# First pair fetched uncast, q pooled one pair ahead, filler matmuls and a ring of six in a fused attention and gated-unit kernel

## The chip, the cores and the metric

One core of one Trainium2 chip runs the whole program. The metric is the device time of one execution in microseconds (us), the median of several runs.

In the text PE is TensorE, DVE is VectorE, ACT is ScalarE, POOL is GpSimd and SP is SyncE.

## The reference, cut to what matters

```python
# q, k, v: (8 batches, 8 heads, 1152, 64) float32, values about 0.1
q_pool = q.reshape(B, H, S // 2, 2, D).mean(axis=3)            # (8, 8, 576, 64)
attn   = softmax(q_pool @ k.T / sqrt(D))
x      = (attn @ v) laid out as (8, 576, 512)
gate   = sigmoid(causal 5-tap convolution of x along the sequence, per channel)
out    = (gate * (x @ w_val)) @ w_out                           # (8, 576, 512) float32
```

Scores are small, so the kernel expands the softmax to first order: per head it needs a 64x64 product of k and v (a Gram matrix) and column sums, not the scores. A flag computed at the end sends the program to an exact version if the inputs are too large. That never happens here.

## The kernel before

Heads are handled in 32 pairs, four pairs to a batch. I call the work for one pair a **slot**, numbered 0 to 31. Slot n computes the Gram matrix of pair n, x of pair n-1, and a quarter of the gated unit ("MoE" in the names) of the batch before. So slots 0 to 3 have no MoE work, and slot 4 is the first full one. "First slot of a batch" below means slots 4, 8, 12 and so on, "second slot" 5, 9, 13 and so on.

```python
def load_pair(n):                 # ring of NKV = 7; GpSimd's DMA casts float32 to bf16
    t = kvs[n % NKV]
    nc.gpsimd.dma_start(out=qn, in_=q[...])
    nc.gpsimd.dma_start(out=t[:, W:2 * W]..., in_=k[...])
    nc.gpsimd.dma_start(out=t[:, 0:W]..., in_=v[...])
# ... (cut)
def pool_q(n):                    # DVE: sum of neighbouring rows of q
    nc.vector.tensor_tensor(out=qp, in0=qv[..., 0, :], in1=qv[..., 1, :], op=ALU.add)
def transposes(n):                # PE: 6 transposes of qp into qt_ps; ACT: copy to mq
    ...
    nc.scalar.copy(out=mq[:, 2 * D:]..., in_=qt_ps...)
# ... (cut)
pool_q(0); transposes(0); setup_conv(); pool_q(1)
for n in range(NPAIR):
    # loads up to pair n + 6; w_val and w_out behind pair 3
    grams(n)                      # PE: sm (18 matmuls), then g (18 matmuls)
    rows(n)                       # DVE
    if late is not None:
        gval(*late)               # DVE: gate times value, left over from slot n-1
    if after:
        xhat(n - 1); xevac(n - 1) # PE; ACT
    rank1(n)                      # PE, needs rows(n)
    if after: norms(n - 1, g)     # PE
    if n >= 2: tap(n - 2, 2)      # DVE: third tap of the convolution
    stat(n, g)                    # DVE
    # ACT: scaled copy of g to mq
    if n >= 2: gate(n - 2)        # ACT: sigmoid
    if moe: mA = val(...) if slot < 2 else outs(...)      # PE
    if n + 2 < NPAIR:
        pool_q(n + 2)             # DVE: two pairs ahead
    if moe: gval(...) if slot < 2 else oevac(...)         # DVE; ACT
    if n + 1 < NPAIR: transposes(n + 1)                   # PE, ACT
    if after: conv(n - 1); tap(n - 1, 0); tap(n - 1, 1)   # PE; DVE
    squares(n)                    # ACT
    if moe: mB = val(...) or outs(...)   # PE; in slot < 2 its gval becomes "late"
```

Each engine executes its instructions in this order.

## Time and profile before

The median is 185.86 us (185.73 to 186.06, 3 runs). The profiled execution took 185.47 us, a little less than these; its span, from the first to the last instruction, is 183.6 us.

| stage of the kernel before | from, to (us) | what sets its pace |
|---|---|---|
| slots 0 to 3 | 9.83 to 33.66 | arrival of the pairs, and the wait for q |
| slot 4, at half clock | 33.66 to 39.43 | PE |
| slots 5 to 31, 18.4 us per batch | 39.43 to 164 | PE |
| tail: last batch of MoE, stores, flag | 164 to 183.6 | PE, then the last stores |

A line of a timeline has the start, the duration, engine, source line, operation and tiles; the bracket is the idle time of that engine just before, and what ended it.

### The profile page before, as it was taken

The page shows a single profiled execution, that of the slowest core. Times are in us where ns is not written, and L with a number is a line of the kernel's source. Part 1 is how long each engine was busy: PE and PEld are TensorE (multiplying, and loading weights), DVE is VectorE, ACT ScalarE, POOL GpSimd, SP SyncE. Part 2 cuts the span into 40 slices and gives each one's busy share as a digit, 9 for nine tenths or more (in the row PEclk, how much of TensorE's full clock was granted, in tenths as well). Part 3 has the DMA queues.
Part 4 walks back from the last instruction along what each step waited for, and adds up shares of the span by engine and source line. Part 5 has one row for each costly group of instructions (what it writes and reads, how often), then busy time and mean ns, then how long its engine had stood idle before and what let it go on. Part 6 is the DMA issues. An engine that isn't in the chain of part 4 may idle for free.

```text
span 183.6 us, 5468 instructions
## 1 busy us (share of the span) xinstructions
PE 156.9 (85%) x2317; PEld 114.4 (62%) x2317; DVE 126.4 (69%) x266; ACT 109.3 (60%) x193; POOL 85.4 (47%) x132
## 2 busy tenths in 40 slices
PE   0269742999999999999999999999999999999910
PEld 0257531787678767876787668867886788657300
DVE  2432606689678967896789669967896789565530
ACT  2124371466886688668866876697569766982210
POOL 7944424444545544444445444455444448672000
PEclk9999985599999999999999999999999999999996
DMA  3999999999999999999999999999999999999340
GB/s 60 176 204 206 207 207 207 207 207 207 206 208 211 205 206 207 208 207 207 207 207 208 207 207 207 208 206 208 207 207 207 223 379 363 367 355 314 146 153 7
DMA packets 28280, 39.23 MB, mean 214 GB/s; under 512 B 2101, under 2 KB 25653, under 8 KB 28250
## 3 DMA queue, kind: packets, MB, share of 16 engines
q0 software_dynamic: 27584, 37.63, 105.5%
q1 hardware_dynamic: 666, 1.19, 1.8%
q8 instruction: 20, 0.33, 0.7%
q14 instruction: 10, 0.08, 0.1%
HBM read 58.73 MB, written 9.44 MB: 371 GB/s over the span
## 4 chain that ended last, share of the span: by engine, by line
PE 76%; DMA 12%; POOL 2%; DVE 2%; issue 2%; ACT 1%; POOLq 0%; DVEq 0%
PE ops L314 19%; PE vps L299 17%; DMA qn<-in_q_dram 12%; PE sm L198 10%; PE cps L261 8%; PE g L198 8%; PE xh L239 6%; PE qt_ps L181 4%; PE g L219 3%; DVE acc L276 1%; POOL kv L101 1%; POOL qn L98 1%; PE g L211 1%; POOL kv L99 0%; DVE acc L271 0%
## 5 line engine op out<-in xcount | busy, mean ns | idle before, releaser
L276 DVE SCALAR_TENSOR_TENSOR acc<-x,convw_sb,acc 128x576 f32<-128x576 bf16 x62 | 50.4, 813 | 1.1
L245 ACT ACTIVATE x<-xh,stats 128x576 bf16<-128x576 f32 x32 | 23.7, 741 | 38.2 <-PE xh L239 38.2
L314 PE MATMUL ops<-wout_sb,gv 128*128 128x512 bf16 (+1 forms) x160 | 39.8, 380 | 0.3 <-DVE gv L305 0.3
L271 DVE SCALAR_TENSOR_TENSOR acc<-x,convw_sb,cps 128x576 f32<-128x576 bf16 x31 | 25.2, 812 | 18.8 <-PE cps L261 11.6
L299 PE MATMUL vps<-x,wval_sb 128*128 128x288 bf16 x256 | 36.7, 285 | 0.2 <-ACT gate L285 0.2
L99 POOL DMA_DIRECT2D kv<-in_k_dram x32 | 23.0, 720 | 28.5 <-DMA kv<-in_v_dram 7.0
L98 POOL DMA_DIRECT2D qn<-in_q_dram x32 | 20.7, 648 | 28.8 <-DMA kv<-in_k_dram 7.9
L198 PE MATMUL sm<-kv,first 128*64 128x128 bf16 x576 | 24.5, 232 | 6.4 <-DMA kv<-in_v_dram 3.5
L198 PEld LDWEIGHTS <-first 128*64 128x64 bf16 x576 | 20.7, 117 | 14.5 <-issue 11.1
L172 DVE TENSOR_TENSOR qp<-qn 96x768 bf16<-96x768 bf16 x32 | 17.5, 547 | 16.4 <-DMA qn<-in_q_dram 16.4
L101 POOL DMA_DIRECT2D kv<-in_v_dram x32 | 23.0, 718 | 10.8 <-DMA qn<-in_q_dram 8.4
L299 PEld LDWEIGHTS <-wval_sb 128*128 128x128 bf16 x256 | 23.7, 97 | 6.7 <-issue 0.7
L305 DVE TENSOR_TENSOR gv<-vps,gate 128x576 bf16<-128x576 f32 x32 | 24.0, 752 | 4.6 <-PE vps L299 4.6
L329 ACT COPY osb<-ops 128x512 f32<-128x512 f32 (+2 forms) x31 | 21.1, 681 | 7.6 <-PE ops L314 7.5
L229 ACT ACTIVATE sq<-mq 128x640 bf16<-128x640 bf16 x32 | 24.0, 750 | 0.0
L198 PE MATMUL g<-kv 128*64 128x128 bf16 x576 | 24.0, 230 | 0.0
L186 ACT COPY mq<-qt_ps 128x576 bf16<-128x576 bf16 x32 | 20.5, 642 | 5.4 <-PE qt_ps L181 5.0
L314 PEld LDWEIGHTS <-gv 128*128 128x128 bf16 (+1 forms) x160 | 14.1, 99 | 14.6 <-issue 2.2
L261 PE MATMUL cps<-x,diag 128*128 128x288 bf16 x128 | 22.0, 295 | 0.1
L323 POOL DMA_DIRECT2D out_dram<-osb x28 | 16.6, 597 | 11.1 <-ACT mq L186 2.1
L283 ACT ACTIVATE gate<-acc 128x576 bf16<-128x576 f32 x31 | 21.0, 679 | 0.4 <-DVE acc L276 0.4
L198 PEld LDWEIGHTS <-kv 128*64 128x64 bf16 x576 | 20.4, 117 | 0.0
(58 smaller groups left out, 130.0 us busy)
## 6 DMA issues: line engine op xcount, KB each, us to landing
qn<-in_q_dram POOLq DMA_DIRECT2D x32, 288.0 KB, 11.0
kv<-in_k_dram POOLq DMA_DIRECT2D x32, 288.0 KB, 10.9
kv<-in_v_dram POOLq DMA_DIRECT2D x32, 288.0 KB, 11.4
out_dram<-osb POOLq DMA_DIRECT2D x7, 512.0 KB, 6.7
out_dram<-osb POOLq DMA_DIRECT2D x14, 256.0 KB, 6.6
out_dram<-osb SPq DMA_DIRECT2D x4, 256.0 KB, 2.0
out_dram<-osb POOLq DMA_DIRECT2D x7, 128.0 KB, 6.2
wval_sb<-in_moe_w_val_dram POOLq DMA_DIRECT2D x1, 512.0 KB, 12.2
```

Of the source, the lines that this page charges most:

```text
L98: nc.gpsimd.dma_start(out=qn, in_=q[b, h0:h0 + 2].rearrange("h (p s) d -> p h (s d)", p=QP))
L99: nc.gpsimd.dma_start(out=t[:, W:2 * W].rearrange("p (h x) -> p h x", h=2), in_=k[b, h0:h0 + 2].rearrange("h (p t) d -> p h (t d)", p=128))
L101: nc.gpsimd.dma_start(out=t[:, 0:W].rearrange("p (h x) -> p h x", h=2), in_=v[b, h0:h0 + 2].rearrange("h (p t) d -> p h (t d)", p=128))
L198: nc.tensor.matmul(out=o, lhsT=first if first_lhs else kvv[:, 1, h, t, :], rhs=kvv[:, :, h, t, :], start=(t == 0), stop=(t == NT - 1), ski ...
L229: nc.scalar.activation(out=sq, in_=mq[:, D:], func=AF.Square)
L245: nc.scalar.activation(out=x[:, PAD:].rearrange("p (c n) -> p c n", c=2), in_=xhs.pop(n)[:, :, 0:HALF], func=AF.Identity, bias=stats[:, n, ...
L261: nc.tensor.matmul(out=cps[:, half, 0:HALF], lhsT=m, rhs=x[:, c0:c0 + HALF], start=(i == 0), stop=(i == len(mats) - 1))
L271: nc.vector.scalar_tensor_tensor(out=acc.rearrange("p (c n) -> p c n", c=2), in0=x[:, kk:kk + Sq].rearrange("p (c n) -> p c n", c=2), scal ...
L276: nc.vector.scalar_tensor_tensor(out=accs[n], in0=x[:, kk:kk + Sq], scalar=convw_sb[:, ft, kk:kk + 1], in1=accs[n], op0=ALU.mult, op1=ALU.add)
L299: nc.tensor.matmul(out=vps[:, half, 0:HALF], lhsT=wval_sb[:, fi, ft * 128:(ft + 1) * 128], rhs=x[:, c0:c0 + HALF], start=(fi == 0), stop=( ...
L305: nc.vector.tensor_tensor(out=gv.rearrange("p (c n) -> p c n", c=2), in0=vps[:, :, 0:HALF], in1=gates.pop(b * NP + ft).rearrange("p (c n) ...
L314: nc.tensor.matmul(out=ops[0:tn, i, :], lhsT=gvs[b, ft][:, t0:t0 + tn], rhs=wout_sb[:, ft, :], start=(ft == 0), stop=(ft == NFT - 1))
```

## The change

The intent was a shorter start: pair 0 comes sooner through the hardware queues; DVE no longer waits for a q that is two pairs away; PE is kept warm by matmuls on a zero tile. The uncast k and v of pair 0 take two places of the ring, which shrinks to six.

```diff
-    NKV = 7
+    NKV = 6
...
+    q0 = [q_pool.tile([QP, 2 * U * D], FP32, name="q0", tag="qn") for _ in range(2)]
+    k0 = kv_pool.tile([128, 2, NT * D], FP32, name="k0", tag="kv")
+    v0 = kv_pool.tile([128, 2, NT * D], FP32, name="v0", tag="kv")
+    for h in range(2):
+        nc.sync.dma_start(out=q0[h], in_=q[0, h]...)
+    nc.scalar.dma_start(out=k0, in_=k[0, 0:2]...)
+    nc.sync.dma_start(out=v0, in_=v[0, 0:2]...)
...
-    load_pair(0)
+    load_pair(1)
...
-    load_pair(1)
+    load_pair(2)
+    idle = consts.tile([128, 512], BF16, name="idle")
+    nc.vector.memset(idle, 0.0)
...
+    def warm(m):        # m matmuls of 128x512 on the zero tile
...
+    warm(12)
     pool_q(0)
     transposes(0)
+    kv0 = kv_pool.tile([128, 2 * W], BF16, name="kv", tag="kv")
+    nc.vector.tensor_copy(out=kv0[:, W:2 * W], in_=k0...)
+    nc.scalar.copy(out=kv0[:, 0:W], in_=v0...)
     setup_conv()
-    pool_q(1)
...
-        while nload < min(NPAIR, n + AHEAD):
+        while nload < min(NPAIR, n + AHEAD - (n < 2)):
...
+        else:                      # slots without MoE work
+            warm(4)
-        if n + 2 < NPAIR:
-            pool_q(n + 2)
+        if n + 1 < NPAIR:
+            pool_q(n + 1)
...
+        else:
+            warm(3)                # end of the slot
```

More of the change, by code (lines that the diff above doesn't have):

```diff
@@ L72, in first_order @@
     TOK = [(t, min(128, Sq - t)) for t in range(0, Sq, 128)]
-    NKV = 7
+    NKV = 6
     consts = ctx.enter_context(tc.tile_pool(name="consts", bufs=1))
-    kv_pool = ctx.enter_context(tc.tile_pool(name="kvp", bufs=1))
+    kv_pool = ctx.enter_context(tc.tile_pool(name="kvp", bufs=NKV))
     q_pool = ctx.enter_context(tc.tile_pool(name="qp", bufs=NKV))
@@ L85, in first_order @@
     ps_b = ctx.enter_context(tc.tile_pool(name="ps_b", bufs=3, space=PSUM))
-    kvs = []
-    for i in range(NKV):
-        t = kv_pool.tile([128, 2 * W], BF16, name=f"kv{i}", tag=f"kv{i}")
-        kvs.append(t)
-    loaded = []
+    kvs, loaded = {}, {}
     def load_pair(n):
@@ L95, in load_pair @@
         h0 = 2 * hp
-        t = kvs[n % NKV]
+        t = kv_pool.tile([128, 2 * W], BF16, name="kv", tag="kv")
         qn = q_pool.tile([QP, 2, 2 * U * D], BF16, name="qn", tag="qn")
@@ L102, in load_pair @@
                             in_=v[b, h0:h0 + 2].rearrange("h (p t) d -> p h (t d)", p=128))
-        loaded.append(qn)
+        kvs[n], loaded[n] = t, qn
+    q0 = [q_pool.tile([QP, 2 * U * D], FP32, name="q0", tag="qn") for _ in range(2)]
+    k0 = kv_pool.tile([128, 2, NT * D], FP32, name="k0", tag="kv")
+    v0 = kv_pool.tile([128, 2, NT * D], FP32, name="v0", tag="kv")
+    for h in range(2):
+        nc.sync.dma_start(out=q0[h], in_=q[0, h].rearrange("(p s) d -> p (s d)", p=QP))
+    nc.scalar.dma_start(out=k0, in_=k[0, 0:2].rearrange("h (p t) d -> p h (t d)", p=128))
+    nc.sync.dma_start(out=v0, in_=v[0, 0:2].rearrange("h (p t) d -> p h (t d)", p=128))
     wval_sb = consts.tile([128, NFT, Dm], BF16, name="wval_sb")
@@ L168, in pool_q @@
     def pool_q(n):
-        qn = loaded[n]
         qp = work.tile([QP, U, 2, D], BF16, name="qp", tag="qp")
-        qv = qn.rearrange("p h (u e d) -> p h u e d", u=U, e=2)
-        nc.vector.tensor_tensor(out=qp.rearrange("p u h d -> p h u d"), in0=qv[:, :, :, 0, :],
-                                in1=qv[:, :, :, 1, :], op=ALU.add)
+        qpv = qp.rearrange("p u h d -> p h u d")
+        if n == 0:
+            for h in range(2):
+                qv = q0[h].rearrange("p (u e d) -> p u e d", u=U, e=2)
+                nc.vector.tensor_tensor(out=qpv[:, h], in0=qv[:, :, 0, :], in1=qv[:, :, 1, :], op=ALU.add)
+        else:
+            qv = loaded.pop(n).rearrange("p h (u e d) -> p h u e d", u=U, e=2)
+            nc.vector.tensor_tensor(out=qpv, in0=qv[:, :, :, 0, :], in1=qv[:, :, :, 1, :], op=ALU.add)
         qps[n] = qp
@@ L189, in grams @@
     def grams(n):
-        kvv = kvs[n % NKV].rearrange("p (c h t d) -> p c h t d", c=2, h=2, t=NT)
+        kvv = kvs.pop(n).rearrange("p (c h t d) -> p c h t d", c=2, h=2, t=NT)
         sm = ps_t.tile([128, 2, D], FP32, name="sm", tag="ts")
@@ L363, in bound_flag @@
         nc.vector.tensor_scalar(out=flag, in0=fin[:, 3:4], scalar1=lim, scalar2=None, op0=ALU.is_le)
+    def warm(m):
+        wps = ps_b.tile([128, 2, 512], FP32, name="wps", tag="big")
+        for _ in range(m):
+            nc.tensor.matmul(out=wps[:, 0, :], lhsT=idle[:, 0:128], rhs=idle, start=True, stop=True,
+                             skip_group_check=True)
     OUTA, OUTB = {2: [0, 1], 3: [3]}, {2: [2], 3: [4]}
-    nload = 2
+    nload = 3
     AHEAD = NKV
+    warm(12)
     pool_q(0)
     transposes(0)
+    kv0 = kv_pool.tile([128, 2 * W], BF16, name="kv", tag="kv")
+    nc.vector.tensor_copy(out=kv0[:, W:2 * W], in_=k0.rearrange("p h x -> p (h x)"))
+    nc.scalar.copy(out=kv0[:, 0:W], in_=v0.rearrange("p h x -> p (h x)"))
+    kvs[0] = kv0
     setup_conv()
-    pool_q(1)
     late = None
@@ L428, in first_order @@
                 oevac(b, OUTB[slot], mB)
+        else:
+            warm(3)
     n, b = NPAIR - 1, B - 1
```

## The prediction

> **What bounds the kernel now.** I read the page's 40 slices first, then the chain of waits that ended last, then the timeline of the first 45 us and the waits, because the diff touches little outside the start. Below are four rows of the page (PE, granted PE clock, DMA share, GB/s by slice of 4.59 us).
>
> ```profile
> PE   0269742999999999999999999999999999999910
> PEclk9999985599999999999999999999999999999996
> DMA  3999999999999999999999999999999999999340
> GB/s 60 176 204 206 207 207 207 207 207 207 206 208 211 205 206 207 208 207 207 207 207 208 207 207 207 208 206 208 207 207 207 223 379 363 367 355 314 146 153 7
> ```
>
> PE is full from slice 7 (about 34 us) to the end; before that it is mostly idle. The DMA engines are full from slice 1 on, with loads at 207 GB/s (bf16 written, twice that read) until about 145 us, then stores. So there are two stages: up to 34 us the kernel waits for data; from 34 us PE is the bound: in the chain, batches of four slots follow each other every 18.4 us (slot starts 53.50 and 71.89 us) and PE has no gap. Everything after 34 us is a fixed length of PE work, so the change is worth what it moves the first full slot (pair 4, the first with MoE work).
>
> The timeline from 29 us, start and duration first, idle time before in brackets:
>
> ```profile
> 29.06 0.56 DVE L172 TENSOR_TENSOR qp<-qn 96x768 bf16<-96x768 bf16 x1 [6.23 <-DMA qn<-in_q_dram]
> ...
> 31.45 0.27 PE L211 MATMUL g<-rows 64*64 64x64 bf16 x2 [3.63 <-DVE rows L204]
> ...
> 32.55 0.72 POOL L99 DMA_DIRECT2D kv<-in_k_dram  x1 [0.81 <-PE qt_ps L181]
> ...
> 33.66 1.17 PE L198 MATMUL sm<-kv,first 128*64 128x128 bf16 x18 [0.25 <-ACT mq L186]
> ...
> 39.43 0.69 PE L198 MATMUL sm<-kv,first 128*64 128x128 bf16 x18
> ```
>
> In slot 2 the in-order DVE sits 6.23 us in the pooling of q for pair 4, two pairs ahead; behind it wait the taps and the rows of slot 3, so PE waits 3.63 us in slot 3. Slot 4 starts at 33.66. Its 18 `sm` matmuls take 1.17 us, against 0.69 for slot 5's: PE is at half clock. Slot 4 lasts 5.77 us; the same kind of slot at full clock lasts 4.39 (57.89 - 53.50 in the chain).
>
> But removing the q wait does not free 6 us, since pair 4's own v lands late. The queue holds eight loads: each issue waits for the load eight before it. The issue at 32.55 is the one that waits for v of pair 4 (the releaser PE named there is an inference); issues come 0.27 us after the landing they wait for (q of pair 4 released DVE at 29.06 and POOL at 29.33), so v of pair 4 landed at about 32.28, only 1.4 us before slot 4 started. By the same reading pair 5 is complete at 36.5 and pair 6 at 41.0, about 4.35 us per pair. Slot 4 can't start before the pair is there: **the start is bound by the DMA stream first**, then by the q wait, then by the cold clock.
>
> **What the Trainium skill says.**
> 1. "DMA: Bandwidth & Descriptors", Issuing engines are not separate DMA queues: DMAs from scalar, sync and gpsimd run on the same 16 engines and interleave. This trace agrees as far as it goes: the share is at its ceiling (1.19 over windows of 5 us) from 10 us on. So the hardware queues cannot add bandwidth, only an earlier start.
> 2. Same page, SWDGE vs HWDGE vs iDMA: only GpSimd's loads can cast; hence the uncast tiles and the on-chip casts here.
> 3. "TensorE: Matmul & The Clock Gate", What you observe / What's actually happening: PE runs at half clock until a busy window of some 3.4 us, and falls back after an idle one. The trace agrees in size: granted clock 1.00 to 26.4 us, 0.50 from 29.8 to 36.6, then 0.98.
> 4. "VectorE: DVE Perf Modes": an fp32 copy between SBUF tiles can run at twice the rate. I use it only to call the k cast short; no row here has its size.
>
> **The change part by part.**
>
> *Pair 0 through hardware queues.* The byte order of the stream is otherwise unchanged: pairs 1 to 3, weights, pair 4. Before, the DMA share is 0.44 in 0 to 5 us and 1.14 in 5 to 10; (0.44 x 5 + 1.14 x 5) / 1.19 = 6.6 us of full work, so the stream starts in effect at 10 - 6.6 = 3.4 us. A sync-queue DMA issued at 0.82 us (that of convw) can have data moving earlier: the final stores land in 2.0 us for 256 KB, of which 0.7 is transfer at 370 GB/s, so data flows within 1.3 us, or from 1.9: a head start of about 1.5 us. Against it, pair 0 as fp32 is 1.77 MB written; at the stores' 360 to 375 GB/s that is 4.8 us, instead of 4.35 with cast: -0.45. So all later pairs land about **1.0 us** earlier (estimate, 0.3 to 1.5).
>
> *The casts.* k0 on DVE, 128x1152: below 1.3 us; v0 on ACT about 1.2 (a 128x1024 fp32 copy there takes 1.01). Two fp32 q poolings, about 0.5 each. All before slot 0's grams, which move to perhaps 10.5 from 9.83. Slots 0 to 3 are waiting for arrivals anyway, so this is hidden by slot 2.
>
> *q one ahead.* DVE in slot 2 no longer waits for q4, nor in slot 3 for q5. Slot 3 starts at about 23.3 (pair 3's copy of mq after the 1.28 us table load) rather than 25.72, then waits for q4 at about 28.1. Transposes, conv and fillers end by 30.6 to 31.8, before or near the arrival of pair 4. The q wait leaves the path.
>
> *Fillers.* 12 at the start, 4 + 3 in each of slots 0 to 3; at full clock one costs about what a 128x512 matmul of L314 takes to issue, 0.22 us (8 in 1.75), so 7 cost 1.5 us in slots that have over 2 us idle: free if PE is warm, up to 1.3 us for the last three if it is cold, just before slot 4. Their use is to have slot 4 start warm: 5.77 - 4.39 = 1.38 us.
>
> *Ring of six.* A load is issued when grams of six pairs back are done: 6 x 4.6 = 27.6 us of room, against 11 us from issue to landing, 1.2 us of grams and a lead of 1 us at slot 5, some 10 at the end. Not binding. Held stores are released one slot later in program order, but the queue, not the slot, sets their time.
>
> Sum: slot 4 starts at 32.28 - 1.0 + 0.15 = 31.4; warm, slot 5 starts at 31.4 + 4.39 = 35.8, against 39.43: gain 3.6 us. The wait for q4 leaves PE idle near 2 us in slot 3; in half of the cases I expect it to fall to half clock, with 0.9 us lost in slot 4: -0.45. From slot 5 on all is shifted. **185.86 - 3.15 = 182.7 us.**
>
> **The rivals.**
> *(a) Arrival keeps everything:* the fp32 pair takes as much as the head start gives. Then slot 4 starts at 32.4: gain 2.6 warm, 1.5 cold: 183.3 to 184.4. For it: fp32 writes twice the bytes. Against: the idle DMA of the first 3 us is real.
> *(b) All works, no cold slot:* gain up to 4.1 with 1.5 us of head start: 181.8. Pairs 5 and 6 land only 0.2 to 0.3 us ahead of their slots, so more isn't possible.
> *(c) The tail collides:* stores run near 316 GB/s to 170 us and the last five start at 172; PE done 3.5 us sooner meets the end of the held stores. The stream also ends 1 us earlier, so at most some tenths are lost.
> *(d) Slower:* the ring of six starves PE, or DVE's setup (casts plus 2.0 us of diagonals) delays slots 1 to 4. The room above speaks against both: 4%.
>
> **Range and chances.** 2% is 3.7 us, just above the undisturbed sum of 3.6; so faster by over 2% only if the head start exceeds 1.1 us and PE stays warm: 33%. Gain 1.5 to 3.7: within 2%, 63%. Range 181.4 to 184.3.
>
> **What would show it.** In the changed profile: slot 4 (first grams followed by vps) starts at 31 to 32; DVE has no wait above 4 us on q in slot 2; the `sm` group of slot 4 takes 0.7 rather than 1.17 us; the granted clock has no 0.5 slices, or only one near slice 6; PE gapless after; load GB/s still 207; the last part after PE's end unchanged. I am wrong if pair 4 lands before 30 or after 32.3, if PE shows DMA waits after slot 5, or if stores hold the end.

## More of the kernel before

In the second slot of a batch DVE has two `gval` products: the late one of the first slot and its own. In the third it has only the late one, in the first only its own.

In the chain of work that ended last, shares of the span by engine read as follows before the change:

```profile
PE 76%; DMA 12%; POOL 2%; DVE 2%; issue 2%; ACT 1%; POOLq 0%; DVEq 0%
```

DVE has 2% of the chain, although it is busy for 69% of the span and for 15.29 of the 18.40 us of a full batch (60.00 to 78.40). It has little slack, but hardly anything waits for it.

The second slot of a batch (slot 9) in the timeline of the kernel before, DVE and PE only and most PE lines left out, becomes important later:

```profile
57.82 0.69 PE L198 MATMUL sm<-kv,first 128*64 128x128 bf16 x18
...
58.60 0.28 DVE L204 TENSOR_TENSOR rows<-sm,rowf 128x128 bf16<-128x128 f32 x1
58.80 0.75 DVE L305 TENSOR_TENSOR gv<-vps,gate 128x576 bf16<-128x576 f32 x1
59.46 0.81 DVE L276 SCALAR_TENSOR_TENSOR acc<-x,convw_sb,acc 128x576 f32<-128x576 bf16 x1
60.19 0.16 DVE L224 COPY stats<-g 128x11 f32<-128x11 f32 x1
60.27 0.55 DVE L172 TENSOR_TENSOR qp<-qn 96x768 bf16<-96x768 bf16 x1
60.47 0.42 PE L181 MATMUL qt_ps<-ident,qp 96*128 96x96 bf16 x6
...
62.31 0.69 PE L198 MATMUL sm<-kv,first 128*64 128x128 bf16 x18
```

The transposes `qt_ps` start at 60.47, 2.65 us after the slot's start, while DVE is still working on a `qp`, which runs from 60.27 to 60.82. That is no conflict: this `qp` is for the pair after next, and the one being transposed was pooled a slot earlier.

## The result, and the profile after

The changed kernel takes **184.56 us** (median; 184.28 to 184.92, 4 runs) against 185.8 for the kernel before in the same rounds. The ratio is 0.9932, 95% interval 0.9909 to 0.9954. The change is worth 0.7%: real, within 2%, and the time is 1.9 us above the predicted 182.7, just outside the stated range.

The same four rows of the page for the changed kernel (PE, granted PE clock, DMA share, GB/s, 40 slices):

```profile
PE   7469986999999999999999999999999999999920
PEclk9957999999999999999999999999999999999996
DMA  5999999999999999999999999999999999999350
GB/s 196 280 208 207 205 208 207 207 207 209 205 210 205 207 207 207 207 207 207 207 207 207 208 206 207 207 207 207 207 207 207 230 385 345 362 333 328 140 171 7
```

The loads start earlier (196 and 280 GB/s in the first two slices, where the uncast pair counts with twice the bytes of a cast one), the half-clock stretch at 27 to 37 us is gone, and PE is busier before slot 4, in part with fillers. All three were intended. The 5 and 7 in the clock row, at 9 to 18 us, are no new loss: there the row of the kernel before shows 9, but its `sm` groups of slots 0 to 2 take 1.17, 1.17 and 1.11 us, which is the half-clock duration. The start of slot 4 in the changed timeline:

```profile
27.93 0.56 DVE L184 TENSOR_TENSOR qp<-qn 96x768 bf16<-96x768 bf16 x1 [0.22 <-DMA qn<-in_q_dram]
...
31.54 0.69 PE L209 MATMUL sm<-kv,first 128*64 128x128 bf16 x18 [1.42 <-DMA kv<-in_v_dram]
...
36.02 0.69 PE L209 MATMUL sm<-kv,first 128*64 128x128 bf16 x18
```

DVE waits 0.22 us for q of pair 4 instead of 6.23. Slot 4 begins at 31.54 when v of its pair lands, runs at full clock (0.69 rather than 1.17 us for its first group), and slot 5 begins at 36.02 instead of 39.43: **3.41 us gained**.

But the chain of work that ended last now reads, by engine:

```profile
PE 51%; DMA 24%; DVE 14%; issue 3%; POOL 2%; ACT 1%; DVEq 0%; POOLq 0%
```

DVE went from 2% to 14%. (DMA's share doubled as well: the start now hangs on v of pair 4, from 17.27 to 31.40 us, and ahead of slot 31 the chain passes through two stores, although slot 30 lasts 5.20 us with and without the change.) The chain in order of time shows where, once per batch (columns: start, length, what):

```profile
52.15 1.02 PE vps L310 x8
53.20 0.76 DVE gv L316
...
54.02 0.82 DVE acc L282
54.87 0.82 DVE acc L287
55.69 0.20 DVE rows L215
55.89 0.66 DVE gv L316
56.55 0.72 DVE acc L287
57.27 0.08 DVE stats L235
57.35 0.48 DVE qp L184
...
57.88 0.43 PE qt_ps L192 x6
```

From 53.2 to 57.9 us the chain runs through eight DVE instructions in a row and comes back to PE at the transposes. The same slot 9 in the changed timeline, for comparison with the one shown before:

```profile
54.83 0.69 PE L209 MATMUL sm<-kv,first 128*64 128x128 bf16 x18
...
57.27 0.55 DVE L184 TENSOR_TENSOR qp<-qn 96x768 bf16<-96x768 bf16 x1
...
57.88 0.43 PE L192 MATMUL qt_ps<-ident,qp 96*128 96x96 bf16 x6 [0.23 <-DVE qp L184]
...
58.91 0.81 DVE L282 SCALAR_TENSOR_TENSOR acc<-x,convw_sb,cps 128x576 f32<-128x576 bf16 x1 [0.40 <-PE cps L272]
...
59.72 0.69 PE L209 MATMUL sm<-kv,first 128*64 128x128 bf16 x18
```

The transposes now need the `qp` of this very slot and have to wait for it: they start 3.05 us after the slot's start instead of 2.65. (The bracket counts only 0.23 of these 0.40 us. It starts at the modelled end of the matmuls ahead, and without a wait the next group starts before that end: in the kernel before, the `vps` matmuls end at 60.63 in the timeline and the transposes start at 60.47.) Each slot's start is that of its first `sm` group, read from the timelines; a slot's length is the distance to the next start.

| slot | length before | length after |
|---|---|---|
| 4 (first full slot) | 5.77 | 4.48 |
| 5, 9, 13, 17, 21, 25, 29 (second of a batch) | 4.48 to 4.49 | 4.88 to 4.89 |
| 6, 10, 14 and so on | 5.19 to 5.20 | 5.19 to 5.20 |
| 7, 11, 15 and so on | 4.15 | 4.14 to 4.15 |
| 8, 12, 16 and so on | 4.56 (slot 20: 4.78) | 4.57 to 4.58 |

Seven second slots lose 0.40 us each, 2.8 us in all. Slot 31 starts at 158.95 instead of 159.67 and the last copy of the output at 174.66 instead of 175.39: of the 3.41 us, 0.7 are left (the longer slot 20 of the profile before, 0.22 us, gives a little back). The two profiled executions differ by 0.9 us in span and 1.1 us in time (185.47 and 184.37); the medians differ by 1.2 us, since the profiled execution of the kernel before was 0.3 us faster than its median.

### The profile page after: what moved, and what is told of

It is laid out like the page before. It is cut to its first block, busy times and chain, and to the rows that moved or that the text cites. A ratio compares the mean times of both kernels' runs of the same rounds, so it can differ in the third digit from the quotient of the medians.

```text
span 182.7 us, 5541 instructions
## 1 busy us (share of the span) xinstructions
PE 162.9 (89%) x2338; PEld 114.1 (62%) x2357; DVE 128.5 (70%) x269; ACT 111.0 (61%) x194; POOL 83.3 (46%) x129
## 4 chain that ended last, share of the span: by engine, by line
PE 51%; DMA 24%; DVE 14%; issue 3%; POOL 2%; ACT 1%; DVEq 0%; POOLq 0%
PE ops L325 16%; PE vps L310 8%; DMA kv<-in_v_dram 8%; PE sm L209 6%; DMA out_dram<-osb 6%; DMA kv<-in_k_dram 6%; PE cps L272 5%; PE g L209 5%; DMA qn<-in_q_dram 5%; DVE gv L316 5%; DVE acc L287 5%; PE xh L250 4%; PE qt_ps L192 3%; DVE acc L282 3%; PE g L230 2%
## 5 line engine op out<-in xcount | busy, mean ns | idle before, releaser
L325 PE MATMUL ops<-wout_sb,gv 128*128 128x512 bf16 (+1 forms) x145 | 39.0, 380 | 1.1 <-DVE gv L316 0.3
L95 POOL DMA_DIRECT2D kv<-in_k_dram x31 | 22.5, 727 | 27.4 <-DMA kv<-in_v_dram 8.2
L94 POOL DMA_DIRECT2D qn<-in_q_dram x31 | 20.0, 646 | 28.3 <-DMA kv<-in_k_dram 8.2
L97 POOL DMA_DIRECT2D kv<-in_v_dram x31 | 22.2, 716 | 12.8 <-DMA qn<-in_q_dram 11.2
L209 PEld LDWEIGHTS <-first 128*64 128x64 bf16 x576 | 19.6, 111 | 12.1 <-issue 10.1
L209 PE MATMUL sm<-kv,first 128*64 128x128 bf16 x576 | 23.2, 224 | 3.8 <-DMA kv<-in_v_dram 1.4
L209 PE MATMUL g<-kv 128*64 128x128 bf16 x576 | 22.8, 222 | 0.0
L272 PE MATMUL cps<-x,diag 128*128 128x288 bf16 x128 | 21.0, 285 | 0.0
L209 PEld LDWEIGHTS <-kv 128*64 128x64 bf16 x576 | 19.3, 112 | 0.0
L192 PEld LDWEIGHTS <-qp 96*128 96x128 bf16 x192 | 10.6, 99 | 11.3 <-DVE qp L184 7.2
```

Source lines behind the costliest of these rows:

```text
L95: nc.gpsimd.dma_start(out=t[:, W:2 * W].rearrange("p (h x) -> p h x", h=2), in_=k[b, h0:h0 + 2].rearrange("h (p t) d -> p h (t d)", p=128))
L97: nc.gpsimd.dma_start(out=t[:, 0:W].rearrange("p (h x) -> p h x", h=2), in_=v[b, h0:h0 + 2].rearrange("h (p t) d -> p h (t d)", p=128))
L209: nc.tensor.matmul(out=o, lhsT=first if first_lhs else kvv[:, 1, h, t, :], rhs=kvv[:, :, h, t, :], start=(t == 0), stop=(t == NT - 1), ski ...
L272: nc.tensor.matmul(out=cps[:, half, 0:HALF], lhsT=m, rhs=x[:, c0:c0 + HALF], start=(i == 0), stop=(i == len(mats) - 1))
L325: nc.tensor.matmul(out=ops[0:tn, i, :], lhsT=gvs[b, ft][:, t0:t0 + tn], rhs=wout_sb[:, ft, :], start=(ft == 0), stop=(ft == NFT - 1))
```

## The experiments

**Theory A**: q pooled one pair ahead makes the transposes of a slot wait for a DVE instruction of the same slot, and the second slot of a batch, where DVE has two products, can't deliver it in time. **Theory B**: the long slots come from another part, the ring of six or the new loads. **Theory C**: the wait for q was never on the path at the start. Twelve kernels ran, in three calls of four; each is timed against the kernel before in its own rounds, whose median was 186.22, 186.19 and 185.91 us. All were correct. The last column gives the ratio and its interval.

| kernel | slot 4 starts | slot 5 starts | slot 21 lasts | slot 31 starts | median us | ratio (95%) |
|---|---|---|---|---|---|---|
| before | 33.66 | 39.43 | 4.48 | 159.67 | 185.8 | 1 |
| changed | 31.54 | 36.02 | 4.88 | 158.95 | 184.56 | 0.9932 (0.9909 to 0.9954) |
| q one ahead, alone | 33.27 | 40.34 | 4.89 | 163.26 | 188.61 | 1.0098 (1.0049 to 1.0148) |
| q two ahead again | 34.81 | 39.29 | 4.48 | 159.31 | 185.53 | 0.9963 (0.9908 to 1.0018) |
| switch at slot 16 | 31.68 | 36.17 | 4.48 | 157.43 | 182.50 | 0.9783 (0.9750 to 0.9816) |
| q first in the second slot | 31.76 | 36.24 | 4.48 | 156.34 | 181.79 | 0.9778 (0.9710 to 0.9845) |
| no fillers | 32.59 | 38.24 | 4.89 | 161.13 | 186.69 | 1.0042 (1.0004 to 1.0081) |
| pair 0 by GpSimd | 32.84 | 38.55 | 4.88 | 161.66 | 186.99 | 1.0051 (1.0013 to 1.0089) |
| ring of seven | 31.77 | 36.25 | 4.88 | 159.14 | 184.22 | 0.9895 (0.9855 to 0.9935) |
| q first, w_out later | 30.34 | 34.91 | 4.49 | 155.83 | 181.44 | 0.9768 (0.9725 to 0.9811) |
| changed, again | 31.59 | 36.07 | 4.89 | 158.99 | 184.58 | 0.9926 (0.9899 to 0.9953) |
| q first, sigmoid in place | 31.15 | 36.07 | 4.48 | 156.16 | 181.73 | 0.9764 (0.9736 to 0.9792) |
| q first, again | 31.48 | 35.97 | 4.48 | 156.06 | 181.87 | 0.9776 (0.9749 to 0.9803) |
| q first, w_out later, again | 30.38 | 34.95 | 4.49 | 155.69 | 181.31 | 0.9749 (0.9721 to 0.9776) |

### 1. q one ahead, alone, in the kernel before

```diff
-        if n + 2 < NPAIR:
-            pool_q(n + 2)
+        if n + 1 < NPAIR:
+            pool_q(n + 1)
```

and no `pool_q(1)` ahead of the loop.

> The kernel before with one edit: q pooled one pair ahead. Theory A (the pooling one ahead puts VectorE on TensorE's path: in the second slot of each MoE batch, slots 5, 9, 13 ... 29, the transposes wait for qp and the slot takes 4.89 us instead of 4.49, seven times 0.40 = 2.8 us; at the start it saves about 1.2 us): about 187.3 us, seven slots of 4.9 us. Theory B (one ahead is harmless; the seven long slots come from the ring of six or from the pair 0 loads): 184.6 us and slots of 4.49.

The seven long slots appear (4.88 to 4.89 us) with the ring of seven and all loads on GpSimd. That alone excludes theory B as a necessary cause. The time is longer than expected (188.61 us, the four runs between 187.52 and 189.08): in the profiled execution v of pair 4 landed later, slot 4 started at 33.27, and PE stayed at half clock for most of it (7.07 us long), so nothing was saved at the start. By itself this part of the change makes the kernel slower by 1.0%.

### 2. The changed kernel with q two ahead again

```diff
-        if n + 1 < NPAIR:
-            pool_q(n + 1)
+        if n + 2 < NPAIR:
+            pool_q(n + 2)
```

and `pool_q(1)` ahead of the loop again.

> The changed kernel with q pooled two pairs ahead as before; everything else of the change kept. Theory A: the seven long slots are gone (-2.8 us), but VectorE waits for q of pair 5 in slot 3 and of pair 6 in slot 4 again, so slot 5 starts at 38 to 39 us instead of 36.0: 183.9 to 184.9 us in all. Theory B (long slots from the ring or the loads): slots of 4.89 stay, and with the q wait it is about 187 us. Theory C (the q wait was never on the path at the start): slot 5 still at 36 us, 181.8 us.

The long slots are gone, and slot 5 starts at 39.29, 0.3 us past the expected window. The answers on the waits of DVE in the first 60 us and of PE show the price (columns: waiting, waited for, us in total, times, longest):

```profile
DVE qp L184 <- DMA qn<-in_q_dram: 6.4, 3, 4.8
```

```profile
PE g L222 <- DVE rows L215: 2.8, 1, 2.8
```

DVE stands 4.8 us in front of a q of a later pair, and PE then waits 2.8 us for the rows behind it. So theory C falls: the wait for q was on the path, and one ahead does remove it. The median, 185.53, is above the expected 183.9 to 184.9; the kernel before was 0.4 us slower in these rounds too, and the interval of the ratio includes 1. The four runs fall into two groups, 184.69 and 184.83, which is as expected, and 186.23 and 186.39; the profile is of the second fastest, so what the slower two lost isn't shown.

### 3. One ahead up to slot 16, two ahead from there

```diff
-        if n + 1 < NPAIR:
-            pool_q(n + 1)
+        if n + 1 < NPAIR and n <= 16:
+            pool_q(n + 1)
+        if n + 2 < NPAIR and n >= 16:
+            pool_q(n + 2)
```

> The changed kernel, q one ahead up to slot 16 and two ahead from there on (both are pooled in slot 16). Theory A: slots 17, 21, 25 and 29 fall from 4.89 to 4.49 us, slots 5, 9 and 13 stay: 184.56 - 1.6 = 182.9 us. Theory B: no change, 184.5 us.

Slots 5, 9 and 13 last 4.88 to 4.89 us, slots 17, 21, 25 and 29 last 4.48. Slot 31 starts at 157.43, 1.5 us sooner than in the changed kernel. The long slots follow the pooling distance within one kernel, with the same loads and ring. By slot 16 the loads are ahead of PE far enough that a q two pairs on is there when DVE comes to it.

### 4. q pooled first in the second slot

```diff
         rows(n)
+        early = moe and slot == 1
+        if early:
+            pool_q(n + 1)
         if late is not None:
             gval(*late)
...
-        if n >= 2:
+        if n >= 2 and not early:
             gate(n - 2)
...
-        if n + 1 < NPAIR:
+        if n + 1 < NPAIR and not early:
             pool_q(n + 1)
...
             transposes(n + 1)
+        if early:
+            gate(n - 2)
```

> The changed kernel with q still one ahead, but in the second slot of each batch VectorE pools q right after the rows, ahead of the late gv product, and ScalarE does the sigmoid after the copy of the transposed q. Same loads, same ring. Theory A: the wait of the transposes goes, slots of 4.5 to 4.6: 181.8 to 182.6 us. Theory B: 184.5 us. If A holds but the order only moves the wait (to the copy of q or to outs), the slots stay above 4.7 us: 183.3 to 184.5.

All seven slots last 4.48 to 4.49 us, and the time falls to 181.79. In the chain that ended last DVE has 0% and PE 76%. Nothing was removed from DVE: it does the same work in another order. This is the strongest evidence for theory A. The slot was not long because DVE had too much to do, but because the one result that PE needs in the same slot stood behind a product and a tap that PE needs only later.

### 5. No fillers

```diff
-    warm(12)
     pool_q(0)
...
-        else:
-            warm(4)
...
-        else:
-            warm(3)
```

> The changed kernel without the filler matmuls. If they keep the clock up: slot 3's wait drops the clock to half, slot 4 takes 5.0 to 5.8 us instead of 4.48, slot 5 starts 0.5 to 1.3 us later, 185.1 to 185.9 us against the 184.56 of the changed kernel. If they do nothing: 184.5 us, slot 4 still 4.5.

The fillers are worth more than expected: the time is 186.69 us, where at most 185.9 was expected, and the ratio is 1.0042 instead of 0.9932, about 2.0 us of 186. Slot 5 starts at 38.24 instead of 36.02. The rows of this kernel show the cold start; first the granted clock in 40 slices, then slot 2 in the timeline:

```profile
PEclk9999999999999999999999999999999999999996
```

```profile
21.01 1.17 PE L209 MATMUL sm<-kv,first 128*64 128x128 bf16 x18
```

The clock row claims full speed, but the group takes 1.17 us, which is the half-clock duration; this row can't be trusted here. Half of the loss is slot 4 at half clock (5.65 us, not 4.48). The other half is that slots 1 to 3 are cold as well: slot 3 then ends at 32.59, after pair 4 has landed, instead of waiting for it.

### 6. Pair 0 by GpSimd with cast again

```diff
-    (the loads of q0, k0 and v0, the two casts and pool_q's branch for pair 0)
-    load_pair(1) ... load_pair(2)
+    load_pair(0) ... load_pair(1)
-    nload = 3
+    nload = 2
-        while nload < min(NPAIR, n + AHEAD - (n < 2)):
+        while nload < min(NPAIR, n + AHEAD):
```

> The changed kernel with pair 0 back on the GpSimd queue with cast (no hardware loads, no casts on chip), one pair ahead, fillers and ring of six kept. If the hardware loads only give a head start of 0.9 us to all arrivals: slot 4 starts at 32.3 to 32.6 instead of 31.5, 185.4 to 185.7 us, the seven slots of 4.89 stay. If the fp32 pair eats its head start: slot 4 at 31.5, 184.5 us. Theory B (the loads cause the long slots) would have slots of 4.49: 182.7 us.

The long slots stay, so the loads did not cause them. Slot 4 starts at 32.84, 1.3 us later than in the changed kernel, and slot 5 2.5 us later; the median of 186.99 us is above the expected 185.4 to 185.7. The timeline of this kernel tells why it is more than the head start:

```profile
30.84 0.43 PE L180 MATMUL qt_ps<-ident,qp 96*128 96x96 bf16 x6 [3.49 <-DVE qp L172]
...
32.84 1.17 PE L197 MATMUL sm<-kv,first 128*64 128x128 bf16 x18 [0.42 <-DMA kv<-in_v_dram]
```

The later arrivals lengthen PE's idle time in slot 3 to 3.49 us, the clock falls to half in spite of the fillers, and slot 4 takes 5.71 us. So in this trace the fillers alone did not keep slot 4 warm. By the ratios, starting from experiment 1, which has neither (its ring of seven does not matter, see experiment 7): the loads alone give 1.0098 - 1.0042 = 0.6%, the fillers alone 1.0098 - 1.0051 = 0.5%, both 1.0098 - 0.9932 = 1.7%. This suggests that each is worth about half without the other, but does not show it: the intervals are 0.2 to 0.5% to each side, and by the starts of slot 5 in the profiles (40.34 with neither, 38.24, 38.55 and 36.02 with both) the gains of 2.1 and 1.8 us nearly add up to the 4.3 of both.

### 7. A ring of seven

```diff
-    NKV = 6
+    NKV = 7
```

> The changed kernel with a ring of seven instead of six. Theory A: nothing changes, 184.3 to 184.8 us, the seven slots of 4.89 us stay. Theory B (the smaller ring costs): 181.8 us.

The seven slots of 4.88 to 4.89 us stay, and slot 31 starts at 159.14, no sooner than in the changed kernel. Theory B falls for the ring too. The ratio is a little lower than that of the changed kernel, with overlapping intervals; I make nothing of it.

### 8. q first, and w_out loaded behind pair 5

```diff
             if nload == 4:
                 nc.gpsimd.dma_start(out=wval_sb, ...)
+            if nload == 6:
                 nc.gpsimd.dma_start(out=wout_sb, ...)
```

on top of experiment 4.

> The variant with q pooled first in the second slot, and in addition the load of w_out moved behind pair 5. Pairs 4 and 5 land 2.5 us earlier, pair 6 as before at about 40: slot 4 at 29.5 to 30, but slot 6 can't start before 40.1, against 40.7 before: 0.3 to 0.6 us less than the 0.978 of the variant, a ratio of 0.975, if the stream of loads is now the floor. If the start of slot 4 alone set the end, 2 us less: 0.967.

Slot 4 starts at 30.34, later than the expected 29.5 to 30 but 1.4 us sooner than in experiment 4; slot 5 then lasts 5.22 us, since q and v of pair 6 land no sooner than before, and slot 6 starts at 40.13, as expected of a stream of loads that has become the floor. The median is 0.35 us lower than in experiment 4, in other rounds and with overlapping intervals; run 12 repeats the comparison.

### 9 to 12. The changed kernel and three variants in the same rounds

> The changed kernel itself, once more, so that it stands against the variants in the same rounds: ratio 0.990 to 0.996 as before, seven slots of 4.89 us.

The changed kernel repeats: 0.9926, with the seven long slots.

The second of the four is experiment 4 with ACT's sigmoid left where it was:

```diff
         rows(n)
+        early = moe and slot == 1
+        if early:
+            pool_q(n + 1)
...
-        if n + 1 < NPAIR:
+        if n + 1 < NPAIR and not early:
             pool_q(n + 1)
```

> The changed kernel with q pooled right after the rows in the second slot of each batch, but ScalarE's sigmoid left ahead of the copy of the transposed q. The wait of the transposes goes; the statistics come 0.5 us later on VectorE, so that ScalarE's copy, in order behind the sigmoid, is expected to hold back the next slot's first matmul instead: slots of 4.7 to 4.9 us, ratio 0.986 to 0.994. If only VectorE's order mattered, slots of 4.49 and a ratio near 0.978.

**My expectation was wrong.** The seven slots are 4.48 to 4.49 us and the ratio 0.9764, so moving the sigmoid was unnecessary. The timeline of slot 5 shows it:

```profile
38.73 0.42 PE L192 MATMUL qt_ps<-ident,qp 96*128 96x96 bf16 x6
...
39.81 0.63 ACT L197 COPY mq<-qt_ps 128x576 bf16<-128x576 bf16 x1
...
40.56 0.69 PE L209 MATMUL sm<-kv,first 128*64 128x128 bf16 x18
```

The copy does come late, but it ends at 40.44, 0.12 us before PE is through with the slot's last matmuls. Moving one DVE instruction in one slot of four is the whole repair.

> The variant with q pooled first and the sigmoid after the copy, again: slots of 4.49, ratio 0.976 to 0.981, that is 0.013 to 0.016 below the changed kernel in the same rounds.

It repeats: 0.9776, which is 0.015 below the changed kernel in the same rounds.

> The same with w_out loaded behind pair 5, again: 0.3 to 0.6 us (0.002 to 0.003) below the variant without, if the difference of the single profiles (slot 31 at 155.8 against 156.3) is real.

Slot 31 starts 0.37 us sooner than without the moved load (155.69 against 156.06), and the median is 0.56 us lower; the intervals of the two ratios overlap a little. By its median this is the fastest kernel tried: 0.9749 of the kernel before and, by the means of the same rounds, 1.8% below the changed kernel (0.9749 / 0.9926 = 0.982).

## Why the prediction was right or wrong

- **What bounds the start: right.** The arrival of pair 4 sets the start of slot 4. Predicted 31.4, measured 31.54; in the chain of the changed kernel v of pair 4 lands at 31.40, 0.9 us sooner than the 32.28 inferred for the kernel before, against the estimated 1.0.
- **The q wait leaves the path at the start: right.** DVE's wait for q of pair 4 fell from 6.23 to 0.22 us, and experiment 2 shows that it comes back with two ahead.
- **Slot 4 warm: right, with the discount unneeded.** It took 4.48 us against 4.39 assumed (57.89 and 53.50 are where the chain passes through two slots, not their starts: slot 8 of the kernel before lasts from 53.26 to 57.82, 4.56 us), and 4.48 to 4.49 again in its repetition, in the switch at slot 16 and with the ring of seven, so the 0.45 us deducted for a cold slot did not occur. The fillers as a whole were undersized: 2.0 us in experiment 5 instead of 1.38. The prediction credited them with slot 4 alone and read the clock row as full speed up to 26.4 us; the `sm` groups of slots 0 to 2 took 1.11 to 1.17 us all the same. Rival (a)'s gain of 1.5 us with a cold slot does not follow from its own terms, which give 2.64 - 1.38 = 1.26.
- **Casts and slots 0 to 3: right in effect, not in detail.** The casts take 0.75 us on DVE and 1.15 on ACT. For the first the prediction had used the Trainium skill, "VectorE: DVE Perf Modes", The perf-mode tier table: it lists a copy of fp32 values within SBUF at twice the rate of a `tensor_tensor` on fp32. The trace fits: 1152 fp32 values per partition took 0.75 us, and `gv`, a `tensor_tensor` with half as many, took 0.75 us as well (its types are mixed, so this is no exact test). Slots 0 to 2 start 1.5 to 2.5 us later than before (11.30, 16.57, 20.60), and slot 3 at 25.70 as before and not at 23.3, held by a copy on ACT behind a table load. None of this matters, since slot 4 waits for its pair.
- **Ring and tail: right.** The ring is not binding (experiment 7). The stores do not collide: the last output copy keeps its distance to the start of slot 31.
- **"From slot 5 on all is shifted": wrong. This is the step that failed.** The text predicted a gapless PE after slot 5 and treated everything from there on as fixed PE work. The prediction counted what pooling one ahead takes away (a wait for a transfer) and not what it adds: a dependence of PE on DVE inside the slot. With two ahead, the transposes use a `qp` that is a slot old, and DVE may lag by most of a slot unnoticed. With one ahead they use the `qp` of the same slot. In the second slot DVE must finish rows, a product, a tap and the statistics first, and `qp` comes 0.4 us too late. Seven times 0.40 makes 2.8 us, which takes the predicted undisturbed gain of 3.6 us down to 0.8; the profiles show 0.7 at the start of slot 31 and the medians 1.2. The unneeded discount of 0.45 us happened to make the miss smaller, which is luck. That the change would stay within 2%, at 63% the likeliest outcome, came true, but not for the reason given.

The rivals in the prediction named late arrivals, a starved ring, a slow setup and a collision of stores, but not this one, and none of the three signs for "I am wrong" appeared. Of the signs expected, "PE gapless after" is the one that failed. The page held the warning: DVE was busy 69% of the span with 2% of the chain. Such an engine has slack only as long as nobody asks it for a result at a fixed moment.

What stays open: how v of pair 4 came to land nearly 1 us later in the profiled execution of experiment 1 than in the kernel before. The delay is there from the first pair on: slot 0, which waits for v of pair 0 in both, starts at 10.69 instead of 9.83, although POOL issues the loads of pair 0 at the same times (1.40, 2.17 and 2.91 us). So it comes from the stream of loads itself and not from a later wait for q; whether it is chance one trace can't tell.

## What to carry to other kernels

When a step is moved nearer to its consumer, look not only at the wait that this removes but at what now lies between the two on the in-order engine, in the busiest slot rather than on average. If the shorter distance is only needed during the start, use it only there, or place the step first among that engine's work for the slot: here moving one instruction turned a gain of 0.7% into 2.2 to 2.4%.

## What the Trainium skill lacked or had wrong

- "TensorE: Matmul & The Clock Gate", What's actually happening: the page lets the clock fall after an idle window of about 3.4 us, and does not say how little work makes a window idle. Here much shorter gaps were enough. In the kernel before, PE stood idle for 2.43 us (23.3 to 25.7 us), worked again, and fell to half clock at about 26.5 us; in experiment 1 it fell at about 25.4 us, before the end of a gap of 1.45 us, with one of 0.83 us shortly before. In the changed kernel a gap of 1.42 us ahead of slot 4 was harmless. So the length of one gap does not tell these apart. PE's work in 3.40 us differs: it was busy for 1.22 us before the fall in experiment 1 (22.0 to 25.4), and for 1.82 us in the poorest such stretch around the gap of the changed kernel (28.2 to 31.6). These are single traces; they show no threshold.
- Same page, Seeing it yourself, HAM trace caveats (which calls the trace's records of the clock unreliable): in experiment 5 the granted clock reads 9 tenths or more in every slice but the last, while the `sm` group takes 1.17 us in slots 0 to 4 and 0.69 from slot 5 on. In the kernel before it reads full speed up to its first recorded fall at 26.4 us, while the `sm` groups of slots 0 to 2 take 1.11 to 1.17 us. The page does not say that the row can show full speed over a cold start; the duration of a known group shows it.
